# Two tokens per lane for queries and keys, 32-bit transposes of 16-bit pairs, and global values set by an engine copy

## The chip, the cores and the metric

The kernel runs on one core of one Trainium2 chip. The metric is the device time of one execution in microseconds. The core has a tensor engine for matrix products (PE), a vector engine (DVE), an activation engine (ACT), a general engine (POOL), and a queue engine (SP) that issues the transfers; 16 DMA engines move the data.

## The reference

An attention layer is followed by a mixture of four attention experts. Batch B = 4, 8 heads, S = 768 tokens, head size 64; the model width is 8 x 64 = 512.

```python
scores = scale * np.matmul(q, k.transpose(0, 1, 3, 2))
is_global = pos[None, :] < 8                       # the first 8 keys
is_local = (rel >= 0) & (rel < 96)                 # the last 96 keys
bias = -slopes * where(is_global & ~is_local, 96, abs(rel))
a = softmax(where(is_global | is_local, scores + bias, -1e9))
x = (a @ v), heads side by side: (B, S, 512)

logits = x @ w_gate                                # 4 experts, the best 2 count
for e in range(4):
    q, k, v = x @ wq[e], x @ wk[e], x @ wv[e]
    a = causal softmax(scale * q @ k.T)
    ye = a @ v @ wo[e]
    out += (gate weight of e for each token) * ye
```

## The kernel before

The work is cut into 24 units of 128 tokens, six for each batch. A unit has a first layer and a second layer, and for each it passes through a chain of small steps, each with a short name that the planner uses:

- `ldq`, `ldk`, `ldv` (L519): SP loads 128 tokens x 8 heads x 64 numbers of each input, one token per lane. A run of 64 floats, 256 bytes, is contiguous in memory. `cq`, `ck`, `cv` (L525, L528) cast them to 16-bit (POOL mostly).
- `tq` (L532 to 536): eight 128x128 transposes on PE bring q and k to the layout with the head's dimension on the lanes, two heads side by side. `eq` copies them from PSUM (a 128x1024 copy on DVE).
- `s0`, `s1` (L559): scores of four heads each, with the keys of this unit and of the unit before. `x0`, `x1` (L563): exponentials on ACT. `m0`, `m1` (L568): product with a table of bias factors, on DVE. `z0`, `z1` (L576, L579): weights times values, with a column of ones for the sums. `r`, `n` (L590, L592): reciprocals and scaling to `x16`.
- A unit looks only at its own block and the one before, and the 8 global keys must be seen everywhere. So `kg` and `vg` (L544, L546) keep the first 8 keys and values of a batch, and once a unit's own block has been used, `kp` (L598) and `vp` (L600) overwrite the first 8 keys and values of that block with the global ones, for the next unit. `kp` is a small copy on POOL, `vp` a transfer of 8 KB on SP's queue. `s` of the next unit waits for `kp`, `z` for `vp`.
- `tx`, `ex` (L604 to 611): four transposes of x and their eviction. `pq` (L614) and `pv` (L621): products with the experts' q/k weights and v/gate weights; `eqk`, `ev`, `xr`, `mx`, `wr`, `zi`: evictions and gate weights.
- `s2`, `x2`, `af`, `y2` (L653 to 685): the experts' causal attention over all units of the batch so far, with a mask on POOL. `rz`, `cw`, `n2`: scaling by the gate weights. `tz`, `ez` (L697 to 709): two transposes and an eviction. `po`, `eo`, `so`: the product with `wo`, its eviction on ACT or DVE, the output's transfer.

The order of instructions on each engine is fixed when the kernel is built. A planner (`Stream.run`, L292) keeps a clock for each engine and repeatedly takes the step that can start earliest by its own table of durations (the numbers in braces behind each step), plus a due time `PACE * u + RANK` weighed by `ALPHA`; where a step may run on two engines, `OTHER` is the penalty for the second. Steps that write PSUM take one of two score buffers or one of four others. Every engine then runs its list in order, so an instruction that waits holds up all behind it, and this goes for SP's transfers too. Input buffers are rings: `raw` has four slots, `qk16` three, `qkT` and `V1` four.

After the main path a check of the softmax sums decides whether a slower general path is run (L757); with these inputs it isn't.

Of the kernel before, what the change touches and what calls it, by code (L numbers as in the profile page):

```python
# [8 lines left out]
F32 = mybir.dt.float32  # L9
# [7 lines left out]
P = 128  # L17
# [4 lines left out]
PACE, ALPHA, TURN = 6.00622, 0.000375979, 0.1  # L22
OTHER = {"m0": 3.12, "m1": 3.35, "eqk": 1.71, "ev": 14.02, "eo": 5.29, "kg": -15.22, "kp": 7.23}
RANK = {
    "ldq": 3.09, "ldk": -1.4103, "ldv": 10.549, "cq": 15.151, "ck": -10.082, "cv": -4.5336,
    "tq": -71.653, "eq": 55.538, "kg": 47.24, "vg": 107.76, "kp": -9.0259, "vp": -19.463,
    "s0": -7.8612, "s1": -17.799, "x0": -50.605, "x1": -67.881, "m0": 14.187, "m1": 99.879,
    "z0": -20.335, "z1": -37.532, "r0": -131.8, "r1": -26.257, "n0": 17.285, "n1": 25.757,
    "tx": -57.992, "ex": 9.4907, "pq": -14.609, "eqk": -26.055, "pv": 28.034, "ev": 73.988,
    "xr": 65.128, "mx": 2.1683, "wr": 21.14, "zi": 51.323, "s2": 11.269, "s2+": 19.618,  # L30
    "x2": 60.753, "x2+": 71.931, "af": -92.082, "y2": 41.953, "rz": 30.062, "cw": 42.106,
    "n2": -35.324, "tz": -7.6056, "ez": -136.19, "po": 59.119, "eo": 47.072, "so": -50.942,
}
W_RANK = -47.481, 2.337, 16.829, -53.198, 17.758
# [287 lines left out]
def kernel(  # L322
# [31 lines left out]
    def ring(n, shape, dt, name):  # L354
        return [const.tile(shape, dt, name=f"{name}_{i}") for i in range(n)]

    def copy(e, o, i):
        act.copy(o, i) if e == "ACT" else (dve if e == "DVE" else pool).tensor_copy(o, i)  # L358
# [5 lines left out]
    ident = const.tile([P, P], FH, name="ident")  # L364
# [17 lines left out]
    raw = ring(R, [P, 3, H, Dh], F32, "raw")  # L382
    qk16 = ring(3, [P, 2, H, Dh], FH, "qk16")
    qkT = ring(R, [P, 2, H // 2, P], FH, "qkT")
# [3 lines left out]
    xT = ring(R, [P, nko, P], FH, "xT")  # L388
# [9 lines left out]
    zT = ring(R, [P, E // 2, P], FH, "zT")  # L398
# [59 lines left out]
    def ld(o, i):  # L458
        return lambda e: nc.sync.dma_start(o, i)
# [8 lines left out]
    st.add(("ld", "o"), ld(wo32[:, :, :], moe_wo.rearrange("(a e) d n -> (e d) a n", e=2)),  # L468
# [27 lines left out]
    def unit(u):  # L496
# [5 lines left out]
        def add(name, fn, engines, after=(), stage=None, kind=None, until=(), rows=False):  # L502

            def full(a):
                return a[0] if isinstance(a, tuple) and a[1] is None else a if isinstance(a, tuple) else (a, u)

            st.add((name, u), fn, engines, [x for x in map(full, after) if x in st.ops or not
                                            (isinstance(x, tuple) and isinstance(x[1], int) and x[1] < u)],
                   PACE * u + RANK[stage or name], kind, [full(a) for a in until], rows,
                   stage or name)  # L510

        def c(key):
            return (key, None)
# [4 lines left out]
        def load(n, src):  # L518
            return lambda e: nc.sync.dma_start(raw[i][:, n, :, :],  # L519
                                               src[b, :, rows, :].rearrange("h s d -> s h d"))  # L520

        for n, src in enumerate((q, k, v)):
            add("ld" + "qkv"[n], load(n, src), {"DMA": 1.2}, [("c" + "qkv"[n], u - R)])
        for n in range(2):
            add("c" + "qk"[n], lambda e, n=n: copy(e, qk16[u % 3][:, n, :, :], raw[i][:, n, :, :]),  # L525
                {"POOL": 0.53} if u else ({"POOL": 0.53}, {"DVE": 0.4})[n],
                ["ld" + "qk"[n], ("tq", u - 3)])
        add("cv", lambda e: copy(e, V1[i][:, :, 0:Dh], raw[i][:, 2, :, :]), {"POOL": 0.6},  # L528
# [3 lines left out]
        def tq(e):  # L532
            T["tq", u] = ps = wtile([P, 2, H // 2, P], FH, "tq")
            for s in range(2):
                for p in range(H // 2):
                    nc.tensor.transpose(ps[:, s, p, :], qk16[u % 3][:, s, 2 * p:2 * p + 2, :], ident[:, :])  # L536

        add("tq", tq, {"PE": 0.46}, ["cq", "ck", c("ident")], None, "w", ["eq"])
        add("eq", lambda e: copy(e, qkT[i][:, :, :, :], T.pop(("tq", u))[:, :, :, :]), {"DVE": 0.6},
            ["tq"] + [(n, u - R + a) for a in range(2) for n in ("s0", "s1")])  # L540


        if ri == 0:
            add("kg", lambda e: copy(e, KG[b % 2][:, :, :], qkT[i][:, 1, :, 0:N_G]), {"POOL": 0.12, "DVE": 0.1},  # L544
                ["eq"] + [("kp", w) for w in range(u - 2 * n_rt, u - n_rt)])
            add("vg", lambda e: copy(e, VG[b % 2][:, :, :], V1[i][0:N_G, :, :]), {"POOL": 0.55},  # L546
                ["cv"] + [("vp", w) for w in range(u - 2 * n_rt, u - n_rt)])

        w = 2 * P if ri else P
        for hf in range(2):  # L550
            def s1(e, hf=hf):
                T["s", u, hf] = sc = stile([P, 2, 2, 2 * P], "sc")
                for pr in range(2):
                    p = 2 * hf + pr
                    for prev in range(2 if ri else 1):
                        for par in range(2):
                            L = slice(par * Dh, (par + 1) * Dh)
                            kt = qkT[(u - prev) % R][L, 1, p, :]
                            mm(sc[:, par, pr, prev * P:(prev + 1) * P], lhsT=kt, rhs=qkT[i][L, 0, p, :],  # L559
                               start=True, stop=True)  # L560
# [22 lines left out]
            add(f"s{hf}", s1, {"PE": 0.24 if ri else 0.13}, ["eq"] + ([("kp", u - 1)] if ri else []),  # L583
# [13 lines left out]
        if ri < n_rt - 1:  # L597
            add("kp", lambda e: copy(e, qkT[i][:, 1, :, 0:N_G], KG[b % 2][:, :, :]), {"POOL": 0.12, "DVE": 0.1},  # L598
                [("kg", b * n_rt), "s0", "s1"])
            add("vp", lambda e: nc.sync.dma_start(V1[i][0:N_G, :, :], VG[b % 2][:, :, :]), {"DMA": 0.1},  # L600
                [("vg", b * n_rt), "z0", "z1"])


        def tx(e):  # L604
            T["tx", u] = ps = wtile([P, nko, P], FH, "tx")
            xv = x16[i][:, :].rearrange("p (kp ko) -> p ko kp", ko=nko)
            for ko in range(nko):
                nc.tensor.transpose(ps[:, ko, :], xv[:, ko, :], ident[:, :])

        add("tx", tx, {"PE": 0.23}, ["n0", "n1"], None, "w", ["ex"])  # L610
        add("ex", lambda e: copy(e, xT[i][:, :, :], T.pop(("tx", u))[:, :, :]), {"DVE": 0.35},
            ["tx", ("pq", u - R), ("pv", u - R)])

        def pq(e):  # L614
            T["pq", u] = ps = wtile([P, 4, P], F32, "pq")
            for j in range(4):
                for ko in range(nko):
                    mm(ps[:, j, :], lhsT=wqk[:, ko, j, :], rhs=xT[i][:, ko, :], start=(ko == 0),  # L618
                       stop=(ko == nko - 1))

        def pv(e):  # L621
            T["pv", u] = ps = wtile([P, E * Hd + 2 * E], F32, "pv")
            for ko in range(nko):
                mm(ps[:, :], lhsT=xT[i][:, ko, :], rhs=wvg[:, ko, :], start=(ko == 0),  # L624
                   stop=(ko == nko - 1))
# [48 lines left out]
        add("af", af, {"POOL": 0.59}, ["x20"])  # L674
# [22 lines left out]
        def tz(e):  # L697
            T["tz", u] = ps = wtile([P, E // 2, P], FH, "tz")
            for p2 in range(E // 2):
                nc.tensor.transpose(ps[:, p2, :], z16[i][:, 2 * p2:2 * p2 + 2, :], ident[:, :])  # L700

        def po(e):
            T["po", u] = ps = wtile([P, Dm], F32, "po")
            for p2 in range(E // 2):
                mm(ps[:, :], lhsT=zT[i][:, p2, :], rhs=wo[:, p2, :], start=(p2 == 0),  # L705
                   stop=(p2 == E // 2 - 1))

        add("tz", tz, {"PE": 0.12}, ["n2"], None, "w", ["ez"])
        add("ez", lambda e: copy(e, zT[i][:, :, :], T.pop(("tz", u))[:, :, :]), {"DVE": 0.2},
# [4 lines left out]
        add("so", lambda e: nc.sync.dma_start(out[b, rows, :], o_sb[i][:, :]), {"DMA": 0.7}, ["eo"])  # L714
# [5 lines left out]
    good = const.tile([P, 3], F32, name="good")  # L720
# [18 lines left out]
    def total(e):  # L739
        T["t"] = ps = wtile([1, 1], F32, "pf")  # L740
        for n in range(3):
            mm(ps[:, :], lhsT=good[:, n:n + 1], rhs=ones[:, :], start=(n == 0), stop=(n == 2))

    st.add("total", total, {"PE": 0.3}, ["good0", "good1", "good2", "ones"], PACE * NU + 30.0, "w", ["flag"])
# [12 lines left out]
    with tc.If(n_good < P * NU * (H + E + 1), label="general"):  # L757
        general_path(tc, q, k, v, moe_w_gate, moe_wq, moe_wk, moe_wv, moe_wo, out)
# [35 lines left out]
```

## Time and profile before

| | |
|---|---|
| median of 3 runs | 158.14 us (157.1 to 158.7) |
| the profiled execution | 157.58 us, span 155.8 us |
| granted PE clock | 0.983 of full over the span |
| PE busy | 124.4 us (80%), 2246 products |
| DVE busy | 126.7 us (81%), 438 instructions |
| ACT busy | 111.0 us (71%), 186 |
| POOL busy | 72.0 us (46%), 132 |
| DMA | 80,687 packets, 27.85 MB; 75,632 of them under 512 B |

Busy time is the time in which an engine had at least one instruction under way. Products on PE are pipelined: one of 128 columns is recorded with 216 ns, but eight in a row take 0.62 us. So PE's busy time says less than DVE's. Shares over the span hide that the kernel has a start, a middle and an end with different limits, so stretches are to be read singly. An entry `L358` is the copy helper that many steps share; its tiles' names tell the step.

### The profile page before, as it was taken

To read this page: it belongs to the slowest core of one execution; us is meant where nothing else is said; L and a number is where in the kernel's file an instruction comes from. 1 tells how busy PE (TensorE), PEld (TensorE's weight loads), DVE (VectorE), ACT (ScalarE), POOL (GpSimd) and SP (SyncE) were. 2 spreads that over 40 slices of the span, in tenths; PEclk is the share of its full clock that TensorE was granted. 3 is DMA by queue.
4 is the path that set the end of the run, shared out by engine and by line. 5 is a ranking of instruction groups with operands and counts; after the bars stand their busy time and mean duration, and the time that the engine had idled before them with its cause. 6 is when DMAs were issued, how large, how long until landed. Compare 5 with 4: busy or idle time off the path is not lost.

```text
span 155.8 us, 5666 instructions
## 1 busy us (share of the span) xinstructions
PE 124.4 (80%) x2246; PEld 99.6 (64%) x2246; DVE 126.7 (81%) x438; ACT 111.0 (71%) x186; POOL 72.0 (46%) x132
## 2 busy tenths in 40 slices
PE   0027885959888988998899989999699999999820
PEld 0015774737777767985777876867588788777400
DVE  3228678987999999898899999999699999978710
ACT  4902457646867987889499968996478879999810
POOL 5037433636476655557938465654392321221000
PEclk9999999999999999999999999999999999999985
DMA  2999669899997999998997999995990221232550
GB/s 52 315 222 215 180 201 231 166 203 234 222 215 137 207 251 217 212 199 172 260 230 206 224 232 199 265 210 144 221 186 4 76 76 67 74 135 74 196 208 13
DMA packets 80687, 27.85 MB, mean 179 GB/s; under 512 B 75632, under 2 KB 77328, under 8 KB 80656
## 3 DMA queue, kind: packets, MB, share of 16 engines
q1 hardware_dynamic: 80656, 27.45, 77.7%
q8 instruction: 18, 0.29, 0.9%
q14 instruction: 13, 0.11, 0.3%
HBM read 20.98 MB, written 6.29 MB: 175 GB/s over the span
## 4 chain that ended last, share of the span: by engine, by line
PE 35%; DVE 21%; DMA 20%; POOL 6%; ACT 5%; issue 5%; SPq 4%; POOLq 0%; ACTq 0%; DVEq 0%
DMA raw<-in_q_dram 13%; DMA raw<-in_k_dram 7%; PE pq L618 6%; DVE A L568 5%; POOL qk L358 5%; PE tq L536 5%; PE po L705 4%; PE z L682 4%; PE s L658 4%; DVE qkT L358 4%; PE pv L624 3%; ACT A L563 3%; PE sc L559 3%; DVE QK L358 2%; DVE cw L689 2%
## 5 line engine op out<-in xcount | busy, mean ns | idle before, releaser
L563 ACT ACTIVATE A<-sc 128x1024 f16<-128x1024 f32 (+1 forms) x48 | 44.8, 962 | 16.0 <-PE sc L559 15.8
L662 ACT ACTIVATE A<-s 128x1024 f16<-128x1024 f32 (+1 forms) x48 | 44.0, 929 | 9.1 <-PE s L658 9.0
L358 POOL CAST qk<-raw 128x512 f16<-128x512 f32 x47 | 31.4, 671 | 31.2 <-DMA raw<-in_q_dram 19.2
L568 DVE TENSOR_TENSOR A<-A,M 128x1024 f16<-128x1024 f16 (+1 forms) x48 | 32.8, 690 | 1.6 <-ACT A L563 1.4
L536 PE MATMUL tq<-ident,qk 128*128 128x128 f16 x192 | 16.1, 231 | 16.3 <-POOL qk L358 15.8
L618 PE MATMUL pq<-xT,wqk 128*128 128x128 f16 x384 | 26.2, 223 | 0.9 <-DVE xT L358 0.7
L670 POOL TENSOR_SCALAR_AFFINE_SELECT A<-A 128x512 f16<-128x512 f16 x24 | 16.8, 699 | 18.8 <-ACT A L662 17.7
L618 PEld LDWEIGHTS <-wqk 128*128 128x128 f16 x384 | 23.1, 100 | 2.6 <-issue 0.9
L536 PEld LDWEIGHTS <-qk 128*128 128x128 f16 x192 | 12.2, 103 | 19.3 <-POOL qk L358 18.1
L358 POOL CAST V<-raw 128x512 f16<-128x512 f32 x24 | 16.2, 675 | 12.2 <-DMA raw<-in_v_dram 6.8
L358 DVE COPY qkT<-tq 128x1024 f16<-128x1024 f16 x24 | 16.3, 678 | 4.1 <-PE tq L536 3.9
L576 PE MATMUL z<-V,A 128*128 128x65 f16 x192 | 17.7, 198 | 2.3 <-POOL V L358 0.9
L592 DVE TENSOR_TENSOR x<-z,rall 128x256 f16<-128x256 f32 x48 | 19.2, 412 | 0.0
L358 DVE CAST QK<-pq 128x512 f16<-128x512 f32 x24 | 16.3, 680 | 1.6 <-PE pq L618 1.6
L658 PE MATMUL s<-QK 64*128 64x128 f16 x336 | 16.2, 218 | 1.3 <-DVE QK L358 1.1
L559 PE MATMUL sc<-qkT 64*128 64x128 f16 x192 | 15.2, 226 | 1.9 <-DVE qkT L358 1.0
L576 PEld LDWEIGHTS <-A 128*128 128x128 f16 x192 | 13.7, 100 | 3.8 <-DVE A L568 1.2
L358 ACT COPY o_sb<-po 128x512 f32<-128x512 f32 x24 | 14.4, 606 | 2.2 <-PE po L705 1.3
L579 PE MATMUL z<-V,A 128*128 128x65 f16 x160 | 14.9, 195 | 0.1
L624 PE MATMUL pv<-wvg,xT 128*128 128x264 f16 x96 | 14.8, 276 | 0.0
L559 PEld LDWEIGHTS <-qkT 64*128 64x128 f16 x352 | 10.9, 97 | 5.9 <-issue 2.8
L705 PE MATMUL po<-wo,zT 128*128 128x512 f16 x48 | 14.3, 380 | 0.3 <-DVE zT L358 0.2
(57 smaller groups left out, 197.9 us busy)
## 6 DMA issues: line engine op xcount, KB each, us to landing
raw<-in_k_dram SPq DMA_DIRECT2D x24, 256.0 KB
raw<-in_q_dram SPq DMA_DIRECT2D x24, 256.0 KB
raw<-in_v_dram SPq DMA_DIRECT2D x24, 256.0 KB
out_dram<-o_sb SPq DMA_DIRECT2D x24, 256.0 KB
w<-in_moe_wq_dram SPq DMA_DIRECT2D x1, 512.0 KB
w<-in_moe_wk_dram SPq DMA_DIRECT2D x1, 512.0 KB
w<-in_moe_wv_dram SPq DMA_DIRECT2D x1, 512.0 KB
wo<-in_moe_wo_dram SPq DMA_DIRECT2D x1, 512.0 KB
```

The source lines that it names most:

```text
L358: act.copy(o, i) if e == "ACT" else (dve if e == "DVE" else pool).tensor_copy(o, i)
L536: nc.tensor.transpose(ps[:, s, p, :], qk16[u % 3][:, s, 2 * p:2 * p + 2, :], ident[:, :])
L559: mm(sc[:, par, pr, prev * P:(prev + 1) * P], lhsT=kt, rhs=qkT[i][L, 0, p, :], start=True, stop=True)
L563: act.activation(A1[(2 * u + hf) % (2 * R)][:, :, :, 0:w], T.pop(("s", u, hf))[:, :, :, 0:w], func=Exp, scale=scale1)
L568: eng[e].tensor_tensor(a, a, M[:, hf, :, :, :] if ri else M0[:, hf, :, :, :], op=Alu.mult)
L576: mm(z[:, h % 4, :], lhsT=a[:, par, pr, 0:P], rhs=V1[i][:, h, 0:DV], start=True, stop=not ri)
L592: add(f"n{hf}", lambda e, hf=hf, r1=r1: dve.tensor_tensor(x16[i][:, 256 * hf:256 * hf + 256].rearrange("p (h d) -> p h d", d=Dh), T.pop((" ...
L618: mm(ps[:, j, :], lhsT=wqk[:, ko, j, :], rhs=xT[i][:, ko, :], start=(ko == 0), stop=(ko == nko - 1))
L624: mm(ps[:, :], lhsT=xT[i][:, ko, :], rhs=wvg[:, ko, :], start=(ko == 0), stop=(ko == nko - 1))
L658: mm(sc[:, par, n, :], lhsT=QK2[b % 2][L, ki, 2 + p2, :], rhs=QK2[b % 2][L, ri, p2, :], start=True, stop=True)
L662: act.activation(A2[i][:, :, 4 * ch:4 * ch + m, :], T.pop(("s2", u, ch))[:, :, 0:m, :], func=Exp, scale=scale2)
L705: mm(ps[:, :], lhsT=zT[i][:, p2, :], rhs=wo[:, p2, :], start=(p2 == 0), stop=(p2 == E // 2 - 1))
```

## The change

Queries and keys are handled for two units at once. A lane now takes two neighbouring tokens, so that 128 floats, 512 bytes, are contiguous in one piece of a load; 12 loads each of q and k take the place of 24. The cast writes the two tokens' 16-bit numbers side by side, and a transpose moves such a pair as one 32-bit element, so one transpose does two tokens x two heads x 64. The evicted PSUM tile is read as 16-bit again, and the tokens lie in their natural order. q and k have a transposition and an eviction of their own. `tx` and `tz` move pairs of neighbouring features in the same way, so that `xT` and `zT` hold pairs, and the products after them read every second element; `wo` is loaded with its rows in the matching order. `vp` becomes an engine copy (POOL or DVE). The identity is 32-bit. A small check, run once, moves known bit patterns through a 32-bit transpose and compares them; its count joins the condition for the general path. The planner's constants are other ones, so the whole order of instructions is new, and some steps land on another engine. Loads of v and the output's transfers stay as they were.

```diff
-PACE, ALPHA, TURN = 6.00622, 0.000375979, 0.1
-OTHER = {"m0": 3.12, "m1": 3.35, "eqk": 1.71, "ev": 14.02, "eo": 5.29, "kg": -15.22, "kp": 7.23}
+PACE, ALPHA, TURN = 16.4546, 2.70323e-11, 0.1
+OTHER = {"m0": 18.25, "m1": 5.2, "eqk": 0.13, "ev": 9.38, "eo": 8.58, "kg": 15.27, "kp": 28.08, "vp": 11.58}
...
-    ident = const.tile([P, P], FH, name="ident")
+    ident = const.tile([P, P], F32, name="ident")
...
-    raw = ring(R, [P, 3, H, Dh], F32, "raw")
-    qk16 = ring(3, [P, 2, H, Dh], FH, "qk16")
-    qkT = ring(R, [P, 2, H // 2, P], FH, "qkT")
+    RB = 3
+    rawqk = ring(RB, [P, 2, H, 2, Dh], F32, "rawqk")
+    rawv = ring(R, [P, H, Dh], F32, "rawv")
+    qk16 = ring(RB, [P, 2, H, Dh, 2], FH, "qk16")
+    qkT = ring(RB, [P, 2, H // 2, 2 * P], FH, "qkT")
...
-    xT = ring(R, [P, nko, P], FH, "xT")
+    xT = ring(R, [P, nko // 2, P, 2], FH, "xT")
...
-    zT = ring(R, [P, E // 2, P], FH, "zT")
+    zT = ring(R, [P, P, 2], FH, "zT")
...
+        u0, bl = u - u % 2, u // 2
+        if u == u0:
+            for n, src in enumerate((q, k)):
+                x = "qk"[n]
+                r, h16, tb = rawqk[bl % RB], qk16[bl % RB], qkT[bl % RB]
+                add("ld" + x, lambda e, r=r, n=n, src=src: nc.sync.dma_start(
+                    r[:, n, :, :, :].rearrange("p h j d -> p h (j d)"),
+                    src[b, :, ri * P:(ri + 2) * P, :].rearrange("h (p j) d -> p h (j d)", j=2)),
+                    {"DMA": 2.0}, [("c" + x, u - 2 * RB)])
+                add("c" + x, lambda e, r=r, h16=h16, n=n: copy(
+                    e, h16[:, n, :, :, :].rearrange("p h d j -> p h j d"), r[:, n, :, :, :]),
+                    {"POOL": 1.1} if u else ({"ACT": 0.95}, {"DVE": 0.6})[n],
+                    ["ld" + x, ("t" + x, u - 2 * RB)])
+
+                def tq(e, n=n, x=x, h16=h16):
+                    T["t" + x, u] = ps = wtile([P, H // 2, P], F32, "t" + x)
+                    for p in range(H // 2):
+                        nc.tensor.transpose(ps[:, p, :], h16[:, n, 2 * p:2 * p + 2, :, :].rearrange(
+                            "p h d j -> p (h d j)").bitcast(F32), ident[:, :])
+
+                add("t" + x, tq, {"PE": 0.25}, ["c" + x, c("ident")], None, "w", ["e" + x])
+                add("e" + x, lambda e, n=n, x=x, tb=tb: copy(
+                    e, tb[:, n, :, :], T.pop(("t" + x, u))[:, :, :].bitcast(FH)), {"DVE": 0.6},
+                    ["t" + x] + [(m, u - 2 * RB + a) for a in range(2 + n) for m in ("s0", "s1")])
...
-            add("vp", lambda e: nc.sync.dma_start(V1[i][0:N_G, :, :], VG[b % 2][:, :, :]), {"DMA": 0.1},
+            add("vp", lambda e: copy(e, V1[i][0:N_G, :, :], VG[b % 2][:, :, :]), {"POOL": 0.63, "DVE": 0.22},
                 [("vg", b * n_rt), "z0", "z1"])
...
         def tx(e):
-            T["tx", u] = ps = wtile([P, nko, P], FH, "tx")
-            xv = x16[i][:, :].rearrange("p (kp ko) -> p ko kp", ko=nko)
-            for ko in range(nko):
-                nc.tensor.transpose(ps[:, ko, :], xv[:, ko, :], ident[:, :])
+            T["tx", u] = ps = wtile([P, nko // 2, P], F32, "tx")
+            xv = x16[i][:, :].bitcast(F32).rearrange("p (kp k2) -> p k2 kp", k2=nko // 2)
+            for k2 in range(nko // 2):
+                nc.tensor.transpose(ps[:, k2, :], xv[:, k2, :], ident[:, :])
...
-                    mm(ps[:, j, :], lhsT=wqk[:, ko, j, :], rhs=xT[i][:, ko, :], start=(ko == 0),
+                    mm(ps[:, j, :], lhsT=wqk[:, ko, j, :], rhs=xT[i][:, ko // 2, :, ko % 2], start=(ko == 0),
...
-                mm(ps[:, :], lhsT=zT[i][:, p2, :], rhs=wo[:, p2, :], start=(p2 == 0),
+                mm(ps[:, :], lhsT=zT[i][:, :, p2], rhs=wo[:, p2, :], start=(p2 == 0),
...
+    def pair_values(e):
+        dve.tensor_scalar_mul(tv[:, :], ti[:, :], STEP)
+        dve.tensor_scalar_mul(te[:, :], tl[:, :].to_broadcast([P, P]), STEP)
+
+    def pair_move(e):
+        T["pt"] = ps = wtile([P, P], F32, "pt")
+        nc.tensor.transpose(ps[:, :], tv[:, :].bitcast(F32), ident[:, :])
+
+    def pair_same(e):
+        dve.scalar_tensor_tensor(tr[:, :], T["pt"][:, :].bitcast(I32), 1.0, te[:, :], op0=Alu.mult,
+                                 op1=Alu.is_equal, accum_out=good[:, 3:4])
```

## The prediction

> **What bounds the kernel now.** I read the table of stretches first. Its rows give, for one stretch of the span, the busy time of PE, weight loads, DVE, ACT and POOL with instruction counts, then the granted clock, the DMA engines' mean busy share and GB/s.
>
> ```profile
> 0.00:10.00 10.00, 0.00 (x0) 0.00 (x0) 3.25 (x15) 5.43 (x17) 2.55 (x14) 1.00 0.83 193
> 10.00:24.00 14.00, 11.20 (x137) 9.39 (x138) 9.49 (x21) 5.89 (x9) 7.16 (x13) 1.00 0.93 203
> 24.00:40.00 16.00, 12.15 (x218) 9.42 (x215) 13.88 (x50) 9.71 (x17) 8.41 (x15) 1.00 1.01 213
> 40.00:110.00 70.00, 64.10 (x1216) 52.12 (x1217) 66.48 (x222) 57.54 (x91) 43.25 (x74) 1.00 0.96 209
> 110.00:150.00 40.00, 36.99 (x682) 28.62 (x678) 33.63 (x135) 32.40 (x55) 10.60 (x18) 1.00 0.43 118
> ```
>
> Two things are nearly full from 40 to 110 us: DVE, at 66.48 of 70, and the DMA engines, at 0.96. After 110 the DMA share halves, because the last inputs are in, and PE, DVE and ACT finish the rest. The chain of waits names the loads most often (start, length, what):
>
> ```profile
> 3.01 6.71 DMA raw<-in_q_dram
> ...
> 55.73 4.85 DMA raw<-in_q_dram
> ...
> 116.07 0.62 PE tq L536 x8
> ...
> 148.19 0.30 DVE zT L358
> ```
>
> The chain alone would make this a load-bound kernel: the first unit's transpositions start at 10.4 and unit 23's at 116.1, so the first attention layer advances every 4.6 us. That is what the loads need. From 60 to 70 us, where nearly everything moved is 256-byte packets, 200 GB/s at a share of 0.99 make 16 x 256 x 0.99 / 200 = 20.3 ns per packet; from 130 to 140, with outputs alone, 83 GB/s at 0.23 make 90.8 ns per 2-KB packet. Per unit that is 3072 x 20.3 / 16 = 3.9 us of loads and 0.7 us of output.
>
> ```profile
> 60.00:70.00 10.00, 9.24 (x203) 8.22 (x201) 8.82 (x35) 8.05 (x13) 6.09 (x11) 1.00 0.99 200
> 130.00:140.00 10.00, 9.97 (x186) 7.79 (x184) 8.62 (x36) 9.74 (x19) 2.55 (x4) 1.00 0.23 83
> ```
>
> But an engine that waits for loads would show idle time, and DVE shows hardly any. From 10 us to the end of its last eviction (148.5) it is busy 123.5 of 138.5 us; its 15.0 idle us are 4.5 (10 to 24), 2.1 (24 to 40), 3.5 (40 to 110) and 4.9 (after). While the first layer waited for loads, DVE worked for the second. So the waits of POOL for loads (19.2 us for q, 12.0 for k) are mostly covered, and I take **DVE's work** as the bound: what leaves DVE shortens the kernel, what only makes loads faster does so through those 15 us.
>
> **The change, part by part.** These rows carry the prices (busy, mean ns of one):
>
> ```profile
> L358 DVE CAST QK<-pq 128x512 f16<-128x512 f32 x24 | 16.3, 680 | 1.6 <-PE pq L618 1.6
> L358 DVE COPY KG<-qkT 128x32 f16<-128x32 f16 x4 | 1.7, 429 | 0.1
> L358 POOL CAST qk<-raw 128x512 f16<-128x512 f32 x47 | 31.4, 671 | 31.2 <-DMA raw<-in_q_dram 19.2 <-DMA raw<-in_k_dram 12.0
> L358 POOL COPY VG<-V 8x528 f16<-8x528 f16 x4 | 2.7, 685 | 0.1
> L742 PE MATMUL pf<-ones,good 128*1 128x1 f32 x6 | 0.3, 163 | 0.0
> ```
>
> *DVE.* The instruction lists of both kernels show what the new planner constants move: 7 of the 24 QK evictions go to ACT (7 x 0.680 = 4.76 us), the 4 KG copies to POOL (4 x 0.429 = 1.72), one weight cast to ACT (0.68). Together **7.2 us** leave DVE after 10 us. The evictions of transposes stay: 24 of 128x1024 and 24 each of xT and zT, now read from PSUM as pairs of halves, with the same shapes. The check of the pair move adds two integer scalings and one comparison with a sum, about 1.0 us by the 128x276 rows (0.29, 0.29, then 0.32 by the 128x128 f32 row plus 0.08), and the first k cast doubles (0.43 to 0.69 by the 128x1024 weight cast). These lie in the first 10 us, where DVE is idle for 6.75; without that cover they cost 1.3 us.
>
> *ACT* gets 7 evictions at 0.606 (the o_sb copy), a weight cast and the first q cast at 1.07 (the wo cast): 111.0 + 6.4 = 117.4 us. Up to here nothing of it is on the path, but ACT, with 105.5 us after 10, comes within 6 us of DVE's 116.3. It is next in line.
>
> *POOL.* 47 casts of 512 become 22 of 1024 with writes at every second half-word, a form the trace lacks. Below, 0.671 + 0.47 = 1.14 us each (512 more elements at the slope between a 32-element copy, 0.234, and the cast); above, twice the time per element, 2.7. I take twice the cast, 1.34: 29.5 us against 31.4. The 20 vp copies come from SP's queue to POOL at 0.685 (0.23 to 0.81 by rows of POOL copies): 13.7 us. With KG, POOL goes from 72 to 85 us of about 150, still with 65 spare. The vp wait moves too. On SP, vp waited for z (13.3 and 6.2 us) with loads queued behind it; on POOL the casts, af and kp queue behind it, and PE waits for those. Each such wait was at most 3.3 us, and POOL's 84 idle us cover it, since the casts run a pair ahead. If that cover went, af and then y2 would be late by that much. A gain is possible too, as z of the next unit no longer waits for a transfer. I take 0, with -1 to +3.
>
> *PE.* 336 transposes of 16-bit become 168 of 32-bit, at the row of 8 in 0.62 us (0.216 for one, so 0.058 each): 19.5 us before. No 32-bit transpose is in the trace. Below: 0.058 each, 9.7 us less. Near: the only 32-bit products (L742) show 6 records for 3 instructions, two passes, so 0.116 each and nothing won. Above: the pitch of a 512-column product (0.43 us for two po, 0.215 each) makes 36.1 us, 16.6 more. I take two passes, 0, since it is the one 32-bit row. The second-layer products now read xT at every second element: 0 (as many columns) to double, 384 x 0.056 = 21.5 us; strided weight loads (tx) took 116 ns against 97 to 103 and didn't widen the transposes' pitch, so I take 0.
>
> The trace's 16-bit weight loads keep that pitch. The Trainium skill (TensorE: Matmul & The Clock Gate, Weight-path perf modes) says that fast weight load is off for FP32 operands, and its rate for ordinary weight loads puts 128 columns at about 107 ns. By the rule 168 x 0.107 = 18.0 us, and PE's gain is gone as well; no row here shows a 32-bit load of 128 columns.
>
> *Loads.* On the line between 20.3 ns (256 B) and 90.8 ns (2 KB) a 512-byte packet takes 30.4 ns. q and k of a unit go from 2048 x 20.3 / 16 = 2.60 us to 1024 x 30.4 / 16 = 1.95, and with v and output from 4.6 to 4.0: 15.6 us of DMA time in all, off DVE's path except in its idle time. 8-KB vp transfers off SP add nothing visible.
>
> The trace's line says 25% off per byte. The Trainium skill (DMA: Bandwidth & Descriptors, Why small descriptors are slow) counts beats plus about 3 cycles for a packet, so 19 cycles for 512 B against 22 for two of 256: 14% off, 8.5 us in place of 15.6. Only the profile after can tell.
>
> *The start.* SP's new order is weights (1 MB), two pairs of q and k (2 MB), wv, then the first v. At 50.5 ns per 1-KB packet (same line) that is 4.85 + 7.78 + 1.30 = 13.9 us, against 3.23 + 6.50 = 9.7: the first V cast goes from 13.4 to about 17.6, and the first q lands 1.3 us later. DVE has more to do meanwhile: 4 qkT, 2 half and 3 full mask products (5.9 us) ahead of its first reciprocal, against 3.1. So 4.2 - 2.8 = **1.4 us** lost. With loads no longer at their limit I give back half of the 2.1 idle us of 24 to 40: 1.0.
>
> *Sum* on the profiled execution (157.58 us, span 155.8): 157.6 - 7.2 + 1.4 - 1.0 = 150.8. The median of the three runs stands 0.36% higher (158.14), so **151.3 us**.
>
> **The rivals.**
>
> (B) *The loads were the bound after all.* For it: the chain, the 4.6 us beat. Against: DVE's 95%. Then the first layer runs up to 15 us ahead, v and q are never late, and of the 15.0 idle us some 5 more go, all of 24 to 40's and most of the tail's: 146.
>
> (C) *The gain is lost in the tail.* From 120 to 149 the chain lies on PE, and ACT is busy 9.74 of 10 us from 130 to 140. If the end is set there, DVE's lighter load only makes more idle time, and the lost start counts: 155 to 159, take 157. It would also be so if the waits on POOL ate it.
>
> (D) *32-bit transposes make PE the bound* (slower). Place: tq, tk, tx and tz, on the way to scores and projections. Price: up to 16.6 us more PE (above). PE's idle time after 40 us is 110 - 101.1 = 8.9 us up to 150, of which 0.8 lies behind its last product, so 8.1 can take it up: the end moves by 8.5, to 166. It decides from (19.5 + 8.1) / 168 = 0.16 us each; strided xT reads would reach the same point at 1.4 times their pitch. Against it: two passes in the only 32-bit row.
>
> (E) *The packets stay at 256 bytes.* The new load is 128x8x128 with 512 contiguous bytes, so I give it nothing apart; it would end as (A) or (C).
>
> **How the numbers follow.** A measurement of this kernel can tell about 1% (its three runs span 157.1 to 158.7), so faster means under 156.6 and slower over 159.7. (A) as summed, 148.5 to 154.5 by POOL's -1 to +3 and idle time: 0.50. (B) 144 to 148.5: 0.20. (C) 154.5 to 159.5: 0.12, a third of it under 156.6. (D) 160 to 170: 0.18. Faster 0.50 + 0.20 + 0.04 = 0.74; within 1% 0.08; slower 0.18. The range leaves out D and the lowest of B: 145.5 to 159.5.
>
> **What the profile after would show.** Right: DVE about 121 us and 95% busy in the middle; QK rows of 17 on DVE and 7 on ACT; some 51,000 packets under 1 KB in place of 75,632, at 30 ns; a DMA share of 0.8 or less in the middle; the first z at about 18 us; POOL near 85. A 32-bit transpose pitch over 0.16 us and PE in the chain from the first half on would be D. DVE idle well under 12 us would be B, and idle over 20 with ACT or PE full would be C. The forecast is also wrong if POOL's pair casts take 2 us or more, since then q and k come late to PE in spite of faster loads.

## The result, and the profile after

The changed kernel takes 165.49 us (median of 4 runs, 165.44 to 166.56) beside 158.42 us of the kernel before (4 runs, 157.1 to 160.15): 1.049 times the time before, 95% interval 1.041 to 1.058. It is slower by 7 us; the forecast was 151.3. Times are medians of all executions, while ratios compare only executions within 1.5% of the fastest of their kernel, so the two can differ a little. The profiled execution took 165.52 us, with a span of 163.8. The granted clock is not the reason: executions at 0.97 and at 0.986 took 165.52 and 165.45 us.

The table of stretches of the changed kernel (columns as in the prediction: PE, weight loads, DVE, ACT, POOL, granted clock, DMA share, GB/s):

```profile
0.00:10.00 10.00, 1.12 (x4) 0.82 (x5) 4.17 (x19) 5.43 (x17) 2.61 (x15) 1.00 0.83 230
10.00:24.00 14.00, 8.82 (x97) 6.29 (x96) 9.72 (x15) 9.04 (x10) 8.08 (x13) 0.88 1.20 285
24.00:40.00 16.00, 14.90 (x209) 12.76 (x209) 14.82 (x43) 11.01 (x19) 9.47 (x14) 0.89 0.55 132
40.00:110.00 70.00, 61.10 (x1044) 48.96 (x1041) 67.11 (x206) 52.41 (x86) 48.22 (x67) 1.00 0.84 206
110.00:150.00 40.00, 36.59 (x628) 29.14 (x627) 35.38 (x118) 33.30 (x54) 16.73 (x26) 1.00 0.31 86
...
60.00:70.00 10.00, 8.55 (x157) 6.86 (x156) 9.33 (x25) 7.20 (x13) 6.97 (x10) 1.00 1.01 247
```

In the middle DVE is as full as before (67.1 of 70 us), yet it gets through 206 instructions where it did 222, because some of them take longer. The DMA share fell from 0.96 to 0.84, and ACT and PE have more idle time. From 10 us to its last eviction DVE is now busy 132.6 us, 9.1 more than before, and idle 14.1. The forecast had counted 7.2 us less.

Which instructions grew, the groups by line and shape show (busy us, mean ns of one | idle time before):

```profile
L583 DVE TENSOR_TENSOR A<-A,M 128x1024 f16<-128x1024 f16 x40 | 41.2, 1032 | 1.4 <-ACT A L578 1.2
L359 POOL CAST qk<-rawqk 128x1024 f16<-128x1024 f32 x22 | 29.4, 1339 | 2.0 <-DMA rawqk<-in_q_dram 1.3 <-DMA rawqk<-in_k_dram 0.7
L607 DVE TENSOR_TENSOR x<-z,rall 128x256 f16<-128x256 f32 x48 | 19.2, 409 | 0.1
L359 POOL COPY V<-VG 8x528 f16<-8x528 f16 x20 | 13.4, 671 | 21.0 <-PE z L594 17.2 <-PE z L591 2.3 <-DVE x L607 1.4
L359 DVE CAST QK<-pq 128x512 f16<-128x512 f32 x17 | 11.6, 682 | 0.5 <-PE pq L634 0.5
L705 DVE SCALAR_TENSOR_TENSOR cw<-wr,zi,rall 128x4 f32<-128x4 f32 x24 | 9.8, 407 | 0.2
```

The same groups before:

```profile
L568 DVE TENSOR_TENSOR A<-A,M 128x1024 f16<-128x1024 f16 x40 | 28.9, 730 | 1.0 <-ACT A L563 0.9
L592 DVE TENSOR_TENSOR x<-z,rall 128x256 f16<-128x256 f32 x48 | 19.2, 412 | 0.0
L689 DVE SCALAR_TENSOR_TENSOR cw<-wr,zi,rall 128x4 f32<-128x4 f32 x24 | 7.3, 303 | 0.1
```

The mask product `m`, unchanged in the code, went from 0.730 to 1.032 us; with its 8 smaller ones the 48 take 46.6 us where they took 33.1. `cw`, a product of 4 elements a lane, went from 0.303 to 0.407. `n` (x<-z,rall) and the QK evictions did not move. The two that grew read both operands from SBUF; the two that did not read one of them from PSUM.

The timeline of POOL and then of DVE in the changed kernel (start, length, engine, line, instruction) shows one such product:

```profile
21.39 0.62 POOL L359 COPY V<-VG 8x528 f16<-8x528 f16 x1
21.96 0.20 POOL L359 COPY qkT<-KG 128x32 f16<-128x32 f16 x1
22.12 1.31 POOL L359 CAST qk<-rawqk 128x1024 f16<-128x1024 f32 x1
23.58 0.83 POOL L359 COPY V<-VG 8x528 f16<-8x528 f16 x1
```

```profile
21.77 2.16 DVE L583 TENSOR_TENSOR A<-A,M 128x1024 f16<-128x1024 f16 x1
23.85 0.41 DVE L359 COPY xT<-tx 128x512 f16<-128x512 f16 x1
```

The product starts while POOL is inside a `vp` copy and ends at 23.93, 0.50 us after the third POOL instruction in a row (22.12 + 1.31 = 23.43). It counts as busy for 2.16 us, of which some 1.5 were standing still. Over the whole trace, a full mask product (1024 elements a lane) that starts with no POOL instruction under way takes 0.68 us in both kernels; most of those that start during a POOL instruction take the rest of it and about half a microsecond, and some stand still for the next ones as well. Of the 40 full products 15 started so before and took 0.82 us in the mean; after, it is 25, at 1.25, half of them during a pair cast.

The chain of waits is now made of DVE and PE in place of loads. Its head lines, by line of code, before and after:

```profile
DMA raw<-in_q_dram 13%; DMA raw<-in_k_dram 7%; PE pq L618 6%; DVE A L568 5%; POOL qk L358 5%; PE tq L536 5%; PE po L705 4%; PE z L682 4%; PE s L658 4%; DVE qkT L358 4%; PE pv L624 3%; ACT A L563 3%; PE sc L559 3%; DVE QK L358 2%; DVE cw L689 2%
...
DVE A L583 16%; PE pq L634 7%; ACT A L578 5%; DMA rawqk<-in_q_dram 4%; DVE x L607 4%; DVE qkT L359 4%; DVE cw L705 4%; PE s L674 4%; DVE QK L359 3%; PE pv L640 3%; DVE z L708 3%; DVE xT L359 3%; PE z L698 3%; PE po L720 3%; PE sc L574 3%
```

### The profile page after: what moved, and what is told of

Its sections match the earlier page's. It is cut to its first block, busy times and chain, and to the rows that moved or that the text cites. A ratio compares the mean times of both kernels' runs of the same rounds, so it can differ in the third digit from the quotient of the medians.

```text
span 163.8 us, 5279 instructions
## 1 busy us (share of the span) xinstructions
PE 129.0 (79%) x2081; PEld 102.0 (62%) x2081; DVE 136.9 (84%) x430; ACT 117.0 (71%) x195; POOL 85.8 (52%) x133
## 4 chain that ended last, share of the span: by engine, by line
DVE 43%; PE 33%; ACT 9%; DMA 4%; issue 4%; SPq 1%; POOL 1%; ACTq 0%; DVEq 0%; POOLq 0%
DVE A L583 16%; PE pq L634 7%; ACT A L578 5%; DMA rawqk<-in_q_dram 4%; DVE x L607 4%; DVE qkT L359 4%; DVE cw L705 4%; PE s L674 4%; DVE QK L359 3%; PE pv L640 3%; DVE z L708 3%; DVE xT L359 3%; PE z L698 3%; PE po L720 3%; PE sc L574 3%
## 5 line engine op out<-in xcount | busy, mean ns | idle before, releaser
L678 ACT ACTIVATE A<-s 128x1024 f16<-128x1024 f32 (+1 forms) x48 | 43.0, 930 | 11.0 <-PE s L674 10.9
L583 DVE TENSOR_TENSOR A<-A,M 128x1024 f16<-128x1024 f16 (+1 forms) x48 | 46.4, 971 | 2.5 <-ACT A L578 2.3
L359 POOL CAST qk<-rawqk 128x1024 f16<-128x1024 f32 x22 | 29.4, 1339 | 2.0 <-DMA rawqk<-in_q_dram 1.3
L686 POOL TENSOR_SCALAR_AFFINE_SELECT A<-A 128x512 f16<-128x512 f16 x24 | 18.2, 760 | 22.0 <-ACT A L678 21.9
L359 POOL COPY V<-VG 8x528 f16<-8x528 f16 x20 | 13.4, 671 | 21.0 <-PE z L594 17.2
L591 PE MATMUL z<-V,A 128*128 128x65 f16 x192 | 17.6, 196 | 5.0 <-DVE QK L359 1.4
L591 PEld LDWEIGHTS <-A 128*128 128x128 f16 x192 | 13.8, 99 | 8.0 <-DVE A L583 2.9
L574 PE MATMUL sc<-qkT 64*128 64x128 f16 x288 | 16.1, 228 | 2.3 <-DVE qkT L359 1.8
L359 POOL CAST V<-rawv 128x512 f16<-128x512 f32 x24 | 16.3, 685 | 0.0
L359 ACT COPY o_sb<-po 128x512 f32<-128x512 f32 x24 | 14.1, 599 | 2.9 <-PE po L720 2.1
L594 PE MATMUL z<-V,A 128*128 128x65 f16 x160 | 15.2, 195 | 0.2 <-POOL V L359 0.2
L698 PE MATMUL z<-V,A 128*128 128x65 f16 x336 | 14.3, 193 | 0.1
L720 PE MATMUL po<-wo,zT 128*128 128x512 f16 x48 | 14.1, 380 | 0.1
L674 PEld LDWEIGHTS <-QK 64*128 64x128 f16 x336 | 9.9, 94 | 6.9 <-issue 2.7
L698 PEld LDWEIGHTS <-A 128*128 128x128 f16 x336 | 12.4, 97 | 1.8 <-issue 0.2
```

The lines of the kernel that those rows point to most:

```text
L574: mm(sc[:, par, pr, prev * P:(prev + 1) * P], lhsT=qkt(u - prev, 1)[L, p, :], rhs=qkt(u, 0)[L, p, :], start=True, stop=True)
L583: eng[e].tensor_tensor(a, a, M[:, hf, :, :, :] if ri else M0[:, hf, :, :, :], op=Alu.mult)
L591: mm(z[:, h % 4, :], lhsT=a[:, par, pr, 0:P], rhs=V1[i][:, h, 0:DV], start=True, stop=not ri)
L674: mm(sc[:, par, n, :], lhsT=QK2[b % 2][L, ki, 2 + p2, :], rhs=QK2[b % 2][L, ri, p2, :], start=True, stop=True)
L678: act.activation(A2[i][:, :, 4 * ch:4 * ch + m, :], T.pop(("s2", u, ch))[:, :, 0:m, :], func=Exp, scale=scale2)
L698: mm(z[:, ex, :], lhsT=A2[i][:, ex % 2, n, :], rhs=V2[b % 2][:, ki, ex, 0:DV], start=(j == 0), stop=(j == len(mine) - 1))
```

## The experiments

"After" is the changed kernel, "before" the one before; "order kept" means that each engine's list is the same but for the edit. Ratios are to runs of the kernel before on the same chip, whose median was 157.25 to 158.79 us.

| kernel | us | ratio, 95% interval | mask mean, us |
|---|---|---|---|
| after | 165.49 | 1.049 [1.041, 1.058] | 1.03 |
| after, mask table of half the heads in PSUM | 176.7 | 1.117 [1.108, 1.126] | 0.67 / 0.89 |
| after, pair casts in two halves | 164.98 | 1.048 [1.038, 1.059] | 0.91 |
| before, q and k cast by one instruction | 159.01 | 1.009 [1.004, 1.014] | 0.76 |
| after, no POOL q/k casts from unit 6 on | 156.58 | 0.995 [0.991, 1.000] | 0.80 |
| after, no `vp` | 158.17 | 0.999 [0.995, 1.003] | 0.87 |
| after, neither | 154.47 | 0.981 [0.970, 0.991] | 0.78 |
| after, `vp` by transfer | 165.8 | 1.045 [1.033, 1.057] | 0.80 |
| after, `vp` on ACT, replanned | 168.32 | 1.062 [1.054, 1.070] | 0.93 |
| after, `vp` on ACT, order kept | 160.05 | 1.020 [1.014, 1.026] | 0.82 |
| after, constants of before | 184.21 | 1.165 [1.152, 1.177] | 0.90 |
| before, 7 QK evictions on ACT | 158.6 | 0.995 [0.989, 1.001] | 0.74 |
| before, `vp` on POOL | 154.94 | 0.984 [0.973, 0.996] | 0.77 |
| before, both of these | 156.14 | 0.989 [0.982, 0.995] | 0.81 |
| after, all QK evictions on DVE | 168.36 | 1.070 [1.064, 1.075] | 1.04 |
| after, neither, all QK on DVE | 155.67 | 0.989 [0.982, 0.995] | 0.72 |
| after, first v loads early | 167.67 | 1.072 [1.061, 1.083] | 1.03 |
| after, `vp` on ACT, first v loads early | 162.0 | 1.035 [1.025, 1.045] | 0.83 |

### Is it the second SBUF operand? The mask table in PSUM

```diff
-    st = Stream({"s": 2, "w": 4})
+    st = Stream({"s": 2, "w": 3})
+    MP = psum.tile([P, 4, P], F32, name="MP")     # bias table of heads 0 to 3, put there by two transposes
...
-                eng[e].tensor_tensor(a, a, M[:, hf, :, :, :] if ri else M0[:, hf, :, :, :], op=Alu.mult)
+                if ri and hf == 0:                # a and MP flattened, MP read as 16-bit
+                    dve.tensor_tensor(a, a, MP, op=Alu.mult)
```

> The changed kernel with the bias table of the first half of the heads held in PSUM (one of the four PSUM buffers is given up for it), so that 20 of the 40 full mask products read one tile from SBUF and 20, as before, two; the order is planned anew. Port theory: the products with the table in PSUM take 0.66 to 0.75 us whatever POOL does, with hardly any spread; the other 20 stay at 0.9 to 1.1 us and wait for POOL's casts. A theory that POOL or the transfers slow any DVE work on SBUF data: both groups lengthen alike. Time: 159 to 163 if the missing PSUM buffer costs nothing, more if it does; the two groups' times decide, not the whole.

Its groups, the product with the table in PSUM and the one with the table in SBUF:

```profile
L603 DVE TENSOR_TENSOR A<-A,M 128x1024 f16<-128x1024 f16 x20 | 17.7, 886 | 0.0
L600 DVE TENSOR_TENSOR A<-A,MP 128x1024 f16<-128x1024 f16 x20 | 13.4, 672 | 1.5 <-ACT A L594 1.5
```

With one operand in PSUM the product takes 0.672 us, none of the 20 under 0.652 or over 0.689; its twin in the same execution, with both in SBUF, takes 0.886, up to 1.73. POOL was as often in the way of both: 10 of the 20 with the table in PSUM started during a POOL instruction and took 0.652 to 0.689 us, 11 of the 20 with the table in SBUF did and took 1.06 in the mean. That settles what stretches it: POOL at work while both operands are in SBUF. The kernel's time says nothing here: with a PSUM buffer less and another order, QK evictions alone waited 5.6 us for PE.

### Is it the length of the casts?

Two kernels change the length: after with each pair cast in two halves, before with a unit's q and k in one instruction.

```diff
+                    for g in range(2 if u else 1):
+                        w = H // 2 if u else H
+                        copy(e, h16[:, n, g * w:g * w + w, :, :]..., r[:, n, g * w:g * w + w, :, :])
```

> The changed kernel, with each POOL cast of a q or k pair (1024 numbers, 1.34 us) issued as two casts of four heads (512 numbers, about 0.67 us); the planner's order is kept, and so is the work. Port theory: a mask product on DVE, which reads two SBUF tiles, stands still until the POOL instruction under way has ended; with pieces half as long it waits half as long, so its mean of 1.03 us falls to about 0.85 to 0.9, DVE's busy time from 136.9 to about 130, and the time from 165.5 to about 160. If POOL's second half starts ahead of the waiting product, the mean stays near 1.0 and the time near 165. Order theory (the new planner constants and the later start cost the time): 165 either way.

```diff
+                elif ("c", u) in T:               # the second of cq, ck casts both
+                    copy(e, qk16[u % 3][:, :, :, :], raw[i][:, 0:2, :, :])
```

> The kernel before, with the two POOL casts of a unit's q and k (0.67 us each) issued as one cast of 1024 numbers (about 1.3 us), from unit 1 on; all else and the planner's order are as before. Port theory: the mask product's mean rises from 0.73 us to 0.85 to 1.0, DVE's busy time from 126.7 to 132 to 138, and the time from 158 to 162 to 167. Order theory: the order is the same, so 158 to 159.5, with at most the first cast's wait for the second input.

Halves of 0.840 us are not half of 1.339; POOL works 5 us more, the mask mean falls only to 0.91, and the intervals show no change of the time. In the kernel before, casts of 1.10 us cost 0.9%, not the 162 to 167 us that I expected from length. So the length of one cast explains only a small part, though the first of these runs also added POOL work and is no clean trial of it. What differs after is how much of POOL's work meets a mask product (25 full products at 1.25 us, in place of 15 at 0.82). My reading, not shown by a run of its own, is that casts queue behind `vp`, which waits for `z` (17.2 us in the row above), and come back to back when it is released: 6 of the 25 stood still through more than one POOL instruction, and none of the 15 before.

### How much does each of POOL's parts cost?

The first of these leaves out the q and k casts from unit 6 on, the second the `vp` copies, the third both; order kept.

```diff
-                add("c" + x, lambda e, r=r, h16=h16, n=n: copy(
+                add("c" + x, (lambda e: None) if u >= 2 * RB else lambda e, r=r, h16=h16, n=n: copy(
```

> The changed kernel without the q and k casts on POOL from unit 6 on (the transposes read the casts of earlier pairs, so q and k of later units are wrong; loads go on). 18 casts of 1.34 us leave POOL, 24 us in all. Port theory: with POOL's long instructions gone the mask product falls to 0.75 to 0.8 us after the first 35 us, DVE's busy time to about 125 to 127, and the time to 153 to 157. Order theory: the same order and start, so 162 to 165, less at most what the wait for the casts is worth (POOL waited 2 us for q and k loads, PE hardly for the casts).

```diff
-            add("vp", lambda e: copy(e, V1[i][0:N_G, :, :], VG[b % 2][:, :, :]), ...
+            add("vp", lambda e: None, ...
```

> The changed kernel without the 20 copies that put the global values in place (later units lack their global values); order kept. It takes 13.4 us of work and 19.5 us of waits for z out of POOL's queue, without a transfer in their place. If the waits and the copies in POOL's queue are what pushes its casts into the mask products: mean 0.8 us, DVE 128, time 156 to 159. If the casts' length alone does it: mean 0.95 to 1.0, DVE 134, time 162 to 164.

> The changed kernel without POOL's q and k casts from unit 6 on and without the 20 copies of global values (so later units read stale q and k and lack their global values); order kept. The two runs with one of them left out gained 8.9 and 7.3 us. If both act through the same waits of DVE for POOL, POOL is left with 50 us and the mask product falls to 0.68 to 0.72: DVE 120 to 121, time 150 to 152. If they act apart (casts through q and k coming late, vp through z), also near 149 to 150, but then with DVE above 122 and its idle time down by 3 us or more from 14.

Without casts 8.9 us go, without `vp` 7.3, without both 11.0: the two overlap. The groups without both:

```profile
L583 DVE TENSOR_TENSOR A<-A,M 128x1024 f16<-128x1024 f16 x40 | 30.9, 775 | 1.7 <-ACT A L578 1.5
L705 DVE SCALAR_TENSOR_TENSOR cw<-wr,zi,rall 128x4 f32<-128x4 f32 x24 | 7.0, 292 | 0.2
```

All mask products together fall by 11.3 us and `cw` by 2.8, 14.1 us off DVE for 11.0 us of time. What PE no longer waits for when that work is gone is in the price too, and these runs don't part the two.

Does `vp` belong elsewhere? As a transfer on SP again, and on ACT, first with a new plan, then at its old place in the order:

```diff
+            add("vp", lambda e: nc.sync.dma_start(V1[i][0:N_G, :, :], VG[b % 2][:, :, :]), {"POOL": 0.63, "DVE": 0.22},
...
+            add("vp", lambda e: copy(e, V1[i][0:N_G, :, :], VG[b % 2][:, :, :]), {"ACT": 0.6},
...
+            add("vp", lambda e: copy("ACT", V1[i][0:N_G, :, :], VG[b % 2][:, :, :]), {"POOL": 0.63, "DVE": 0.22},
```

> The changed kernel with the global values put in place by a transfer on SP's queue again, as in the kernel before; the planner's order is kept. Port theory: POOL loses 20 copies of 0.67 us, which are one part in six of its busy time, so the mask product falls from 1.03 to about 0.95 us, and the time to 162 to 164. A theory that the wait for z, which now holds up POOL's queue (19.5 us in all), costs the time: 160 or less. Order theory: 165, or more since SP's loads wait behind the transfer.

> The changed kernel with the global values copied by ACT (0.6 us each by the planner) in place of POOL; planned anew. POOL loses 13.4 us and the waits for z, ACT gets 12 us. Theory that vp in POOL's queue makes half of the loss: mean 0.8 to 0.85, DVE 128 to 130, time 157 to 160, with ACT near 129 us as the next limit. Theory that only the casts matter: mean 0.95 to 1.0, time 163 to 166.

> The changed kernel with the 20 copies of global values on ACT, in the place in the order that they had on POOL (the run that planned anew is spoilt by its other order). Port theory: as without the copies, mask product 0.85 to 0.9, DVE 128 to 130; ACT's 12 us and its waits for z cost a part, so 158 to 162. If a wait for z hurts wherever it is queued, ACT's exponentials come late: 165 or more.

As a transfer it heals the mask (0.80) and gains nothing: DVE's reciprocals now wait 8.7 us for `z`, which, as I read it, waits for the transfer. On ACT with the order kept it gains 5.4 us, though ACT gets 8.5 us more to do. With a new plan it loses 2.8, at a granted clock of 0.96 against 0.99: the same edit differs by 8 us with the order.

### Is it the new order?

After with the planner constants of before:

```diff
-PACE, ALPHA, TURN = 16.4546, 2.70323e-11, 0.1
+PACE, ALPHA, TURN = 6.00622, 0.000375979, 0.1
```

> The changed kernel with the planner constants of the kernel before (the new steps take those of tq, eq and kp). Order theory: the time falls to 155 to 160 with the mask product still near 1.0 us. Port theory: another order of the same work meets POOL as often, the mean stays at 0.9 to 1.1, and the time at 162 to 168.

184.2 us: the new steps with the old constants are far worse. So going back to them mends nothing; that another order of the new steps would do better is not excluded, as the 8 us above show how much an order can be worth.

### Does what leaves DVE shorten the kernel?

The forecast's premise, tried on the kernel before: 7 of 24 QK evictions to ACT, `vp` to POOL, and both.

```diff
-        add("eqk", lambda e: copy(e, QK2[b % 2][:, ri, :, :], ...
+        add("eqk", lambda e: copy("ACT" if u % 7 in (2, 5) else e, QK2[b % 2][:, ri, :, :], ...
```

> The kernel before with 7 of the 24 QK evictions on ACT (units 2, 5, 9, 12, 16, 19, 23), order kept: the part of the change that the forecast counted as its gain, alone. If DVE's work sets the time as the forecast had it: DVE 122, time 152 to 154. If it is the loads or the order: 157 to 159.

```diff
-            add("vp", lambda e: nc.sync.dma_start(V1[i][0:N_G, :, :], VG[b % 2][:, :, :]), ...
+            add("vp", lambda e: copy("POOL", V1[i][0:N_G, :, :], VG[b % 2][:, :, :]), ...
```

> The kernel before with the global values copied by POOL in place of the transfer; order kept. Port theory: POOL's 13.7 us more and the queueing behind z push its casts into the mask products; mean 0.73 to 0.85 or more, DVE 126.7 to 131 or more, time 160 to 163. If the copy is harmless in this order: 157 to 158.5, and a gain is possible since SP's loads no longer wait for z (19.5 us of waits).

> The kernel before with two parts of the change together: vp as POOL copy (alone it gave 154.9) and 7 of 24 QK evictions on ACT (alone 158.6), order kept. Theory: the loads queued behind vp on SP paced the first layer, and only once they are released does DVE's work set the time. Then the evictions, worth nothing alone, are now worth 2.5 to 4.5 us of DVE's work: 150 to 152.5, with DVE idle 10 to 12 us after 10 us. Rival: behind the loads comes not DVE but ACT or PE, or DVE's gaps grow as before by what leaves it: 154 to 156, DVE idle 13 or more.

Moving the evictions alone gains nothing that can be measured: DVE's busy time after 10 us falls by 2.6 us and its idle time rises from 15.1 to 18.0. Taking `vp` off SP alone gains 1.6% (interval 0.4 to 2.7%), the lowest ratio of the kernels that leave nothing out. The stretches of 10 to 24 and 40 to 110 us in that kernel:

```profile
10.00:24.00 14.00, 11.77 (x140) 9.86 (x140) 9.94 (x21) 6.23 (x9) 9.09 (x16) 1.00 1.28 249
...
40.00:110.00 70.00, 64.31 (x1225) 52.67 (x1226) 68.49 (x224) 57.76 (x91) 50.72 (x86) 1.00 0.99 216
```

Early on the loads move 249 GB/s where they moved 203, since they no longer queue behind `vp`'s wait for `z`; DVE then reaches 68.5 of 70 in the middle and its idle time falls to 10.7 us. Part of the wait was on the path, although most of DVE's time was busy. Both edits together give a ratio of 0.989 beside 0.984, with intervals that overlap: no further gain that these runs can show, against my theory.

In the changed kernel the same evictions go back onto DVE, with POOL's work in place and without it:

```diff
-        add("eqk", lambda e: copy(e, QK2[b % 2][:, ri, :, :], ...
+        add("eqk", lambda e: copy("DVE", QK2[b % 2][:, ri, :, :], ...
```

> The changed kernel with all 24 QK evictions on DVE again, order kept: 7 x 0.680 = 4.8 us go back onto DVE. If DVE's time to stand still behind POOL is a fixed cost beside its work, DVE's busy time grows by 4.8 us and the time by 3.5 to 5 us, to 169 to 170.5. Rival: DVE then only arrives later at mask products that would have stood still anyway, and the mask's mean falls from 1.03 to 0.95 or less: 165 to 167.

> The changed kernel without POOL's q and k casts from unit 6 on and without the vp copies (154.5), with all 24 QK evictions on DVE again. It leaves both kinds of work out. Hardly any mask product stands still here, so this prices the moved evictions alone. If DVE's work sets the time of the changed kernel: 157.5 to 159.5. If DVE has room there (idle 16 us): 154 to 156, and the mask's mean stays at 0.78 in both cases.

With POOL's work the kernel gets slower by 2.9 us (ratio 1.070 beside 1.049, intervals apart), and the mask products are as long as they were. Its groups:

```profile
L583 DVE TENSOR_TENSOR A<-A,M 128x1024 f16<-128x1024 f16 x40 | 41.4, 1038 | 1.0 <-ACT A L578 1.0
L359 DVE CAST QK<-pq 128x512 f16<-128x512 f32 x24 | 16.4, 682 | 0.5 <-PE pq L634 0.5
```

So here DVE's work does count, at 2.9 us for 4.8 of work, 0.6 of it and less than I expected. Without POOL's work the difference is 1.2 us with overlapping intervals.

### What does the late start cost?

After, and after with `vp` on ACT, with the v loads of units 0 and 1 issued ahead of the second pair of q and k and of wv. Shown is the order of SP's queue, not the code:

```diff
-SP: wq wk wg | k q (units 0, 1) | k q (units 2, 3) | wv | v 0, v 1 | ...
+SP: wq wk wg | k q (units 0, 1) | v 0, v 1 | k q (units 2, 3) | wv | ...
```

> The changed kernel with one change on SP's queue alone: the v loads of units 0 and 1 go ahead of the second pair of q and k and of wv; all engines keep their order. Theory: DVE is full from 24 us on, so a late start costs in full; the first V cast moves from 19.1 to 15 to 16.5 and the first reciprocal from 20.5 to 17 to 18, and the time falls by 2 to 4 us: 161.5 to 163.5. Rival: the second pair of q and k, 2.6 us later, then keeps PE and DVE waiting by as much: 164.5 to 167 as before.

> The changed kernel with vp on ACT at its place in the order (160.1) and the v loads of units 0 and 1 ahead of the second pair of q and k. If the late start costs in full: 156 to 158. Rival (the second pair is then late by as much, or the start's loss is taken up later): 159.5 to 161.

It went the other way. The first reciprocal came at 23.8 us in place of 20.9, since POOL, PE and DVE have the second pair's work ahead of it in their order and now waited for that pair; the times rose by 2.2 us for 2.9 us, and in the second kernel by 1.9 us for 3.0. The v load was not what the first reciprocal had waited for. In the changed kernel it had landed at 16.7 us; the first V cast then stood behind a `kp` copy on POOL, which waited 2.49 us for scores:

```profile
18.94 0.21 POOL L359 COPY qkT<-KG 128x32 f16<-128x32 f16 x1 [2.49 <-PE sc L574]
19.09 0.62 POOL L359 CAST V<-rawv 128x512 f16<-128x512 f32 x1
```

The edit was meant to shorten the start and lengthened it, yet it gives a price: some 0.7 us of time for each us that the first reciprocal is late. That is a rough estimate, since in the runs above that keep both the order and the loads the first reciprocal came anywhere from 20.7 to 22.4 us in the one profile of each. The second kernel's ratio just overlaps with that of its counterpart, the first one's doesn't.

## Why the prediction was wrong

**The step that failed: "7.2 us leave DVE".** The removals are there (17 QK evictions on DVE, KG on POOL), but the sum kept the mask product at its 0.730 us while the same text put 13 us more on POOL and made its casts twice as long. The mask products took 13.5 us more and `cw` 2.5: 16.0 us came onto DVE while 7.2 left. That POOL's work can cost DVE time was nowhere among the terms or the rivals. The PSUM experiment shows the cause, the runs without casts and without `vp` its size. I read POOL as an engine with "65 spare" and took `vp` there as 0, with -1 to +3; leaving it out gained 7.3.

The trace before held the warning: the 1024-element products were 0.68 us where nothing ran on POOL and up to 1.01 where something did, under one mean of 0.730. The Trainium skill (SBUF — State Buffer, Who interferes with whom) states that a DVE instruction with two SBUF inputs contends with a GpSimd (POOL) instruction that reads SBUF, and that the port pair they share is an exclusive lock. The two mask tables of this case agree: 0.672 with one operand in PSUM, 0.886 beside it with none. It is the rule that spoke against this change, and the prediction left it out.

**The premise "what leaves DVE shortens the kernel"** was false for the kernel before (7 evictions away: ratio 0.995, interval 0.989 to 1.001) and true by 0.6 for the changed one (7 evictions back: +2.9). That DVE was 95% busy in the middle did not mean that its work paced the rest. Part of its 15 us of idle time lay on the path: rival B was partly right, as the gain from `vp` off SP shows. I had set aside the chain of waits, which named the loads most often.

**The start.** Expected: first V cast at 17.6, set by the loads, 1.4 us lost. Measured: 19.1, although its load had landed at 16.7; the first reciprocal came at 20.9 in place of 15.0. At the rough 0.7 this is worth 4.1 us. So the sign was right and the size too small, and the mechanism was another in part: the last 2.4 us before the V cast were no longer a load but POOL's order, with a `kp` copy in front that waited for scores.

**A ledger**, with prices from runs where there are some: the stretched products 16.0 x 11.0 / 14.1 = +12.5; the start +4.1; the QK evictions -2.9; together +13.7. The kernel lost 7.1, so some 6.6 us came back: the other 2.4 us moved off DVE, faster loads, `vp`'s wait off SP. That share is worked out as a remainder and was not measured; the prices also overlap in part, as casts and `vp` did.

**What held.** PE: in `tq` and `tk` a 32-bit transpose follows the one before at 0.109 us, a 16-bit one at 0.056, two passes, as taken (0.116). The second of `tx`'s two came after 0.18 us in the median, so rival D's 0.16 was passed there, but D needed it for all 168. Products with every second element of `xT` keep their pitch (0.056 to 0.057), so 0 was right. The rule that the prediction took from the Trainium skill (TensorE: Matmul & The Clock Gate, Weight-path perf modes), that fast weight load is off for FP32 operands, agrees with the trace: 32-bit weight loads took 0.14 to 0.20 us in the mean against 0.098 for `pq`'s. The 107 ns estimated from the page was too low.

```profile
L634 PEld LDWEIGHTS <-wqk 128*128 128x128 f16 x384 | 23.7, 98 | 4.8 <-issue 3.1
...
L545 PEld LDWEIGHTS tk<-ident,qk 128*128 128x128 f32 x48 | 6.2, 160 | 6.7 <-DVE qk L359 6.2 <-issue 0.2
```

ACT (117.0 against 117.4), POOL (85.8 against 85) and the pair cast (1.339 against 1.34 us) came out as worked out. The loads did as well: from 60 to 70 us, 247 GB/s at a share of 1.01 against 200 at 0.99, 21% more bytes per busy time, and single packets of 512 bytes took 32.3 ns in the mean, 30.4 expected, beside 20.8 for those of 256 bytes in the same trace: 22% off per byte, nearer to the trace's line (25%) than to the 14% of the count of beats in the Trainium skill (DMA: Bandwidth & Descriptors, Why small descriptors are slow). Rival E is out: packets under 512 bytes fell from 75,632 to 25,936. DMA time was no longer the limit (a share of 0.84 in the middle); as I read it, that bought little because DVE took its place.

**Open.** How the 6.6 us of the remainder divide; how much of the 11.0 us is the stretched products and how much PE's shorter waits; why 4.8 us of evictions gain nothing in the kernel before even with its loads released; and how fast the changed kernel would be with all its mask tables in PSUM at no loss of a buffer, which was not tried.

## What to carry to other kernels

An engine's spare time is not free where it shares a path with the bound: before work goes to POOL, look which DVE instructions read two SBUF operands, split them by whether POOL was busy when they started, and price the rest of a POOL instruction for each that will meet one. A mean in which some instances stand still hides both the engine's true work and what more of the neighbour will do to it. And a small transfer that waits on a queue in order is paid by the loads behind it: in this kernel the copy alone, without the rest of the change, was the better half (154.9 us, 1.6% less).

## What the runs showed that I had not expected

- DVE can be kept out across several POOL instructions, not for one only: the longest mask product took 2.5 us, and the one shown above waited through three.
- Small DVE instructions pay as well: `cw`, with 4 elements a lane, grew by 0.10 us in the mean (0.303 to 0.407), in the kernel with the old constants to 0.68.
- In the kernel before, moving 4.8 us of evictions off DVE took only 2.6 us off its busy time; the 48 mask products together grew by 0.9 us. As I read it, they started earlier and stood still longer, and the trace books that as work. One profile shows no more than that.
